# SwiGLU feed-forward on one core: interleaved tokens in the first two tiles, and the order of TensorE's waits

## The chip, the cores and the metric

The kernel runs on one core of a Trainium2 chip. The metric is the device time of one execution in microseconds (us), as a median of runs. A profile is one execution recorded by the hardware; its span goes from the first to the last instruction.

## The reference

```python
B, S, D, F = 1, 2048, 512, 1376          # x: [B, S, D], all bf16
def reference(x, w_gate, w_up, w_down):
    g = _silu(x @ w_gate)                # [S, F]
    u = x @ w_up
    return (g * u) @ w_down              # [S, D]
```

## The kernel before

The work has two halves. In the first, the hidden dimension stands on the partitions: for each chunk of 512 tokens (four chunks, `c`) and each block of 128 hidden columns (`ft`), one group of four matmuls (`dk`, the four 128-row parts of D) computes the gate, kind "G", and one the up projection, kind "U". The weights are what TensorE loads; x, transposed (`xT_sb`), streams. ScalarE applies silu to a gate group, VectorE multiplies with the up group into `hT_sb`. The 96 hidden columns left over are handled by groups of kinds "X" and "Y". In the second half, kind "O", tokens stand on the partitions: 16 tiles of 128 tokens are multiplied with w_down (matmuls on strips of 32 rows, L442, for most of it, and whole ones, L481, at the end), copied to `o_sb` by VectorE or ScalarE, and stored. There are eight `o_sb` buffers for 16 tiles.

The order on every engine is written out by hand, with semaphores. The part that matters here is the start. TensorE first runs matmuls on constants (`warm`, L354 to L356). The x of the first two tiles of 128 tokens (`NXN` = 2) is loaded plainly, rows on partitions, into `xn_sb` by `load_xn` (L113): xn0 is the first DMA on SP's queue, xn1 the second on ACT's queue, behind the first gate slab wg0. TensorE transposes these two tiles (`transposes`, L362 to L368) and VectorE and ScalarE copy the results to `xT_sb` in turn (parts 0 and 2 on VectorE, 1 and 3 on ScalarE). The x of all later tokens comes transposed by the DMA (`load_x`, L93): x0b and x0c for the rest of the first chunk, then one DMA for each further chunk.

The weights arrive in slabs of hidden blocks: block 0 (wg0, wu0), block 1 (wg1, wu1), blocks 2 and 3 (wg2, wu2), 4 to 6, and 7 to 10. The issue order on SP's queue is xn0, wu0, wg1, wu1, wg2, wu2, x0b, x0c, then the rest. TensorE takes the first eight groups (L370 to L385) in pieces as loads land: the first gate and up group on tokens 0 to 127, then on 128 to 255; then the groups at 2, 3, 4, 6, 5, 7 on tokens 0 to 255 (at 4 and 6 stand the gates of slab wg2, at 5 and 7 the ups of slab wu2); then the upper 256 tokens, which need x0b and x0c.

TensorE's waits go through `need` (L306, a load has landed) and `after` (L313, an operation of ScalarE or VectorE is done). Each weight load can carry a wait; where two stand before one weight load, the second in program order stands as an instruction of its own ahead of it.

Stores (`store_tiles`, L253) follow the order of `tiles` (L232), in which tile 0 is the fourth and tile 1 the eighth.

Of the kernel before, what the change touches and what calls it, by code (L numbers as in the profile page):

```python
# [14 lines left out]
def bass_standalone__swiglu_ffn__prompt_kernel(nc, x, w_gate, w_up, w_down, out):  # L15
    _, S, D = x.shape
    F = w_gate.shape[1]
    P = 128
# [11 lines left out]
    NXN = HT // P  # L30
    NB = 8
    NSG = 4
    NOS = 8
    SR = 32
    T01, T2, TAIL = NFF, NFF + 1, NFF + 2
    NWD = NFF + 3
    Y_ROWS = [0, 64, 0, 64]
# [4 lines left out]
    xf = x[0]  # L42
    of = out[0]
# [7 lines left out]
    with ExitStack() as es:  # L51
# [15 lines left out]
        o_sb = [sb(f"o_sb{i}", [P, D], BF16) for i in range(NOS)]  # L67
# [3 lines left out]
        xn_sb = sb("xn_sb", [P, NXN, D], BF16)  # L71
        ident = sb("ident", [P, P], BF16)

        s_I = sem("s_I")
# [6 lines left out]
        s_out = [sem(f"s_out{i}") for i in range(NOS)]  # L81
        loads = {}

        def load_sem(name):
            loads[name] = sem(f"s_{name}")
            return loads[name]
# [24 lines left out]
            load_w(eng, f"wu{a}", w_up, UPH, a * P, min(b * P, F - 32))  # L111

        def load_xn(eng, i):  # L113
            eng.dma_start(xn_sb[:, i, :], xf[i * P:(i + 1) * P, :]).then_inc(load_sem(f"xn{i}"), 16)

        def out_rows(t):
            return of[t * P:(t + 1) * P, :]

        def loads_on_scalar(act):
            load_gate(act, *slabs[0])  # L120
            load_xn(act, 1)

        def loads_on_sync(sp):
            load_xn(sp, 0)
            load_up(sp, *slabs[0])
            for a, b in slabs[1:3]:
                load_gate(sp, a, b)
                load_up(sp, a, b)
            load_x(sp, "x0b", HT, HT + P)
            load_x(sp, "x0c", HT + P, SC)  # L130
            for a, b in slabs[3:]:
                load_gate(sp, a, b)
                load_up(sp, a, b)
            load_w(sp, "wut", w_up, F - (F - 32), F - 32, F)
            for c in range(1, NSC):
                load_x(sp, f"x{c}", c * SC, (c + 1) * SC)
            sp.dma_start(
                wd_sb[:, 0:NFF, :], w_down[0:NFF * P, :].rearrange("(k p) d -> p k d", p=P)
            ).then_inc(load_sem("wd"), 16)
            load_sem("wdt")  # L140
            for y0 in (0, 64):
                sp.dma_start(wd_sb[y0:y0 + 64, T01, :], w_down[NFF * P:F - SR, :]).then_inc(loads["wdt"], 16)
            for x0 in range(0, P, SR):
                sp.dma_start(wd_sb[x0:x0 + SR, T2, :], w_down[F - SR:F, :]).then_inc(loads["wdt"], 16)
            sp.dma_start(wd_sb[0:F_LAST, TAIL, :], w_down[NFF * P:F, :]).then_inc(load_sem("wdl"), 16)
# [7 lines left out]
        def add_group(kind, **what):  # L153
            g = dict(kind=kind, at=len(groups), bank=banks[len(groups) % NB], readers=[], **what)
            groups.append(g)
            return g

        def add_op(eng, g, **what):
            n_read[eng] += 1
            op = dict(g=g, at=n_read[eng], **what)  # L160
            (act_ops if eng == "A" else dve_ops).append(op)
            g["readers"].append((eng, op["at"]))
            return op

        def tview(i, dk):
            return banks[KD * i + dk][:, 0:P // 2].bitcast(BF16)
# [26 lines left out]
        def plan_x(c):  # L193
# [4 lines left out]
            d = add_op(  # L198
                "D", g, kind="mul", out=hx_sb[X_ROWS[c]:X_ROWS[c] + SR, c, :],
                a=sgx_sb[c][96:128, :], b=g["bank"][96:128, :], after=a["at"] - 1,  # L200
# [12 lines left out]
        xt_ready = {}  # L213
        for i in range(NXN):
            for dk in range(KD):
                eng = "DA"[dk % 2]
# [16 lines left out]
        for at, t in enumerate(tiles):  # L233
            ob = at % NOS
            need = 16 * n_store[ob]
            parts = [(0, D)] if at < NST - 1 else [(0, LASTA), (LASTA, LASTB), (LASTB, D)]
            for c0, c1 in parts:
                g = add_group("O", t=t, c0=c0, c1=c1)
                eng = "A" if at % 2 == 1 and c0 == 0 else "D"
                op = add_op(  # L240
                    eng, g, kind="copy", out=o_sb[ob][:, c0:c1], src=g["bank"][:, 0:c1 - c0],
# [11 lines left out]
        def store_tiles(eng, own):  # L253
            for o, t, c0, c1, ob, copied, n in stores:
                if o == own:
                    eng.wait_ge(s_A if copied == "A" else s_D, n)
                    eng.dma_start(out_rows(t)[:, c0:c1], o_sb[ob][:, c0:c1]).then_inc(s_out[ob], 16)

        def on_sync(sp):
            loads_on_sync(sp)  # L260
            store_tiles(sp, "S")
            for i in range(NOS):
                sp.wait_ge(s_out[i], 16 * n_store[i])
# [11 lines left out]
        def on_scalar(act):  # L275
            loads_on_scalar(act)
            act.activation(adummy[:, 0:4], zero_c, ACT.Silu)  # L277
            for op in act_ops:
                act.wait_ge(*ready(op))
                if op["kind"] == "silu":  # L280
                    if op["free"]:
                        act.wait_ge(s_D, op["free"])
                    fn = ACT.Silu
                else:
                    if op["stored"][1]:
                        act.wait_ge(*op["stored"])
                    fn = ACT.Copy
                act.activation(op["out"], op["src"], fn).then_inc(s_A, 1)  # L288
            store_tiles(act, "A")
# [13 lines left out]
        def on_tensor(pe):  # L303
            landed = set()

            def need(name, count=1):  # L306
                if name not in landed:
                    pe.wait_ge(loads[name], 16 * count)
                    landed.add(name)
# [3 lines left out]
            def after(eng, n):  # L313
                if n > read[eng]:
                    pe.wait_ge(s_A if eng == "A" else s_D, n)
                    read[eng] = n
# [12 lines left out]
            def gu_needs(g, n0, n1):  # L329
                c, ft = g["c"], g["ft"]  # L330
                if c > 0:
                    need(f"x{c}")
                if c == 0 and n1 > HT:
                    need("x0b")
                if c == 0 and n1 > HT + P:
                    need("x0c")
                need(("wg" if g["kind"] == "G" else "wu") + str(slab_of[ft]))

            def gu_step(g, dk, n0, n1):
                c = g["c"]  # L340
                col = (0 if g["kind"] == "G" else UPH) + g["ft"] * P
                if c == 0:
                    for i in range(n0 // P, min(n1 // P, NXN)):
                        after(*xt_ready[i, dk])
                ins = whole(g["bank"], dk, col, c, n0, n1)
                if n1 == SC and dk == KD - 1:
                    ins.then_inc(s_P, 1)

            def gu_matmuls(g, n0, n1):
                gu_needs(g, n0, n1)  # L350
                for dk in range(KD):
                    gu_step(g, dk, n0, n1)

            def warm(n, width):  # L354
                for i in range(n):
                    pe.matmul(banks[NB - 1][:, 0:width], lhsT=ones_w, rhs=ones_m[:, 0:width], start=True, stop=True)  # L356

            warm(N_WARM, SC)
            warm(N_FILL, P)
            pe.wait_ge(s_I, 1)  # L360

            def transposes(i):  # L362
                need(f"xn{i}")
                for dk in range(KD):
                    pe.matmul(  # L365
                        tview(i, dk), lhsT=xn_sb[:, i, dk * P:(dk + 1) * P], rhs=ident[:, :],
                        start=True, stop=True, is_transpose=True,
                    ).then_inc(s_X, 1)  # L368

            first = groups[0:NB]  # L370
            transposes(0)
            warm(N_GAP, P)
            gu_matmuls(first[0], 0, P)
            transposes(1)
            gu_matmuls(first[1], 0, P)
            for dk in range(KD):
                for g in first[0:2]:
                    gu_step(g, dk, P, HT)
            for at in (2, 3, 4, 6, 5, 7):
                gu_matmuls(first[at], 0, HT)  # L380
# [6 lines left out]
            for g in groups[NB:NO]:  # L387
# [4 lines left out]
                elif kind == "X":  # L392
                    c = g["c"]
# [21 lines left out]
            def strip_of(c, k):  # L415
                spare = (P + SR - 2 * Y_ROWS[c] - X_ROWS[c]) // SR
                return (spare + k) % TPC

            def strips(q, k, fks, start, stop, turn=True):
# [7 lines left out]
                for fk in fks:  # L427
                    if fk == NFF:
                        need("wdt", 2 + TPC)
                    for c, g in zip(ORDER, quad):  # L430
                        t, c0, c1 = g["t"], g["c0"], g["c1"]
                        r0 = SR * strip_of(c, k)
                        tok = (t - c * TPC) * P
# [35 lines left out]
            for g in groups[NO + TPC * (TPC - 1):]:  # L469
                t, c0, c1 = g["t"], g["c0"], g["c1"]  # L470
# [17 lines left out]
        on_gpsimd(nc.gpsimd)  # L488
        on_scalar(nc.scalar)
        on_tensor(nc.tensor)  # L490
        on_vector(nc.vector)

# [27 lines left out]
```

## Time and profile before

| | us |
|---|---|
| median of 3 runs | 120.4 |
| the runs | 120.46, 119.94, 120.40 |
| span of the profiled execution | 118.6 |
| TensorE busy in it | 115.9 (98%) |
| VectorE busy | 38.0 (32%) |
| ScalarE busy | 35.1 (30%) |

The page gives no other time of the profiled execution than its span; the runs' times include what lies around the span, 1.8 us by the median. PE in the profile is TensorE's matmuls, PEld its weight loads, which overlap with matmuls; DVE is VectorE, ACT ScalarE, SP the queue that issues most DMAs. A "q" behind an engine's name is its sequencer, which waits and issues and is not counted as busy. The chain of waits follows the end of the span back to what released it. In the tables by stretch, the DMA share is the mean busy share of the 16 DMA engines, and values over 1 mean that packets overlap.

### The profile page before, as it was taken

How to read it: one execution, taken by the hardware profiler on the slowest of the kernel's cores; microseconds unless marked ns; L12 is line 12 of the kernel's file. 1: busy time of each engine (PE TensorE's matmuls, PEld its weight loads, DVE VectorE, ACT ScalarE, POOL GpSimd, SP SyncE). 2: the span in 40 equal slices, each digit the busy share in tenths (PEclk: the TensorE clock that was granted, in tenths of full speed). 3: DMA queues.
4: the chain of work that ended last, by engine and by line, in shares of the span. 5: the costliest groups of instructions: out<-in, count | busy, mean ns of one | idle time of the engine just before them, and what ended most of it. 6: DMA issues, size and time to landing. Idle time of an engine off the chain costs nothing.

```text
span 118.6 us, 2344 instructions
## 1 busy us (share of the span) xinstructions
PE 115.9 (98%) x1019; PEld 59.7 (50%) x1019; DVE 38.0 (32%) x60; ACT 35.1 (30%) x62; POOL 1.1 (1%) x7
## 2 busy tenths in 40 slices
PE   7999999999999999999999999999999999999993
PEld 2788444444444444444444444444444445885442
DVE  0206542444433444324444244360000044003321
ACT  3407334353244272343263432330000033003021
POOL 1000000000000000000000000010000000000000
PEclk9999999999999999999999999999999999999999
DMA  3999999991000000000000000000000017200612
GB/s 87 290 186 336 296 161 221 268 357 25 0 6 0 0 0 0 0 3 3 0 0 6 0 0 0 0 0 6 0 6 0 0 57 237 70 0 6 202 64 88
DMA packets 17642, 8.83 MB, mean 74 GB/s; under 512 B 10624, under 2 KB 17632, under 8 KB 17632
## 3 DMA queue, kind: packets, MB, share of 16 engines
q1 hardware_dynamic: 16816, 8.33, 27.3%
q10 hardware_dynamic: 816, 0.36, 1.1%
q8 instruction: 8, 0.13, 0.5%
q14 instruction: 2, 0.02, 0.0%
HBM read 4.75 MB, written 2.10 MB: 58 GB/s over the span
## 4 chain that ended last, share of the span: by engine, by line
PE 98%; DVE 0%; issue 0%
PE bank L324 62%; PE bank L442 25%; PE bank L481 7%; PE bank L356 2%; PE bank L404 2%; PE bank L365 1%; DVE o_sb L300 0%
## 5 line engine op out<-in xcount | busy, mean ns | idle before, releaser
L324 PE MATMUL bank<-xT_sb,w_sb 128*128 128x512 bf16 (+2 forms) x384 | 73.3, 352 | 0.1
L324 PEld LDWEIGHTS bank<-xT_sb,w_sb 128*128 128x128 bf16 x384 | 36.2, 98 | 36.8 <-DMA w_sb<-in_w_gate_dram 0.3
L296 DVE TENSOR_TENSOR hT_sb<-sg_sb,bank 128x512 bf16<-128x512 f32 x40 | 27.5, 688 | 40.2 <-PE bank L324 39.3
L288 ACT ACTIVATE sg_sb<-bank 128x512 f32<-128x512 f32 x40 | 23.9, 597 | 40.6 <-PE bank L324 40.5
L442 PE MATMUL bank<-wd_sb,hT_sb 32*128 32x512 bf16 x496 | 29.0, 374 | 0.0
L442 PEld LDWEIGHTS bank<-wd_sb,hT_sb 32*128 32x128 bf16 x496 | 15.2, 93 | 11.6 <-issue 0.4
L300 DVE CAST o_sb<-bank 128x512 bf16<-128x512 f32 (+1 forms) x10 | 5.7, 595 | 31.1 <-PE bank L442 25.9
L288 ACT ACTIVATE o_sb<-bank 128x512 bf16<-128x512 f32 (+1 forms) x8 | 4.3, 582 | 33.6 <-PE bank L442 27.9
L481 PE MATMUL bank<-wd_sb,hT_sb 128*128 128x512 bf16 (+2 forms) x56 | 8.1, 304 | 0.0
L481 PEld LDWEIGHTS bank<-wd_sb,hT_sb 128*128 128x128 bf16 x56 | 4.2, 98 | 4.2 <-issue 0.4
L442 PE MATMUL bank<-wd_sb,hy_sb 32*128 32x512 bf16 (+1 forms) x32 | 5.0, 371 | 0.0
L296 DVE TENSOR_TENSOR hx_sb<-sgx_sb,bank 32x512 bf16<-32x512 f32 x4 | 2.8, 692 | 3.5 <-ACT sgx_sb L288 3.5
L288 ACT ACTIVATE sgx_sb<-bank 32x512 f32<-32x512 f32 x4 | 2.4, 588 | 4.5 <-PE bank L324 4.5
L356 PE MATMUL bank<-const-bfloat16-1.0 128*128 128x512 bf16 (+1 forms) x9 | 2.8, 463 | 0.8 <-PEq L505 0.8
L442 PE MATMUL bank<-wd_sb,hx_sb 32*128 32x512 bf16 (+1 forms) x16 | 3.0, 371 | 0.0
L288 ACT ACTIVATE sgy_sb<-bank 64x512 f32<-64x512 f32 x4 | 2.4, 590 | 0.1
L356 PEld LDWEIGHTS bank<-const-bfloat16-1.0 128*128 128x128 bf16 x9 | 1.0, 128 | 2.2 <-issue 2.2
L300 DVE COPY xT_sb<-bank 128x128 bf16<-128x128 bf16 x4 | 0.8, 222 | 4.3 <-PE bank L365 4.3
L404 PE MATMUL bank<-xT_sb,w_sb 128*64 128x512 bf16 x16 | 1.9, 382 | 0.0
L442 PEld LDWEIGHTS bank<-wd_sb,hy_sb 32*128 32x128 bf16 x32 | 1.6, 93 | 0.6
L277 ACT ACT_TABLE_LOAD x1 | 1.3, 1283 | 1.9 <-issue 1.9
L404 PEld LDWEIGHTS bank<-xT_sb,w_sb 128*64 128x64 bf16 x16 | 0.8, 109 | 1.0 <-DVE hT_sb L296 0.4
(15 smaller groups left out, 6.6 us busy)
## 6 DMA issues: line engine op xcount, KB each, us to landing
out_dram<-o_sb SPq DMA_DIRECT2D x15, 128.0 KB, 1.8
wd_sb<-in_w_down_dram SPq DMA_DIRECT2D x1, 1280.0 KB, 7.3
w_sb<-in_w_gate_dram SPq DMA_DIRECT2D x1, 480.0 KB, 5.5
w_sb<-in_w_up_dram SPq DMA_DIRECT2D x1, 448.0 KB, 6.2
w_sb<-in_w_gate_dram SPq DMA_DIRECT2D x1, 384.0 KB, 4.3
w_sb<-in_w_up_dram SPq DMA_DIRECT2D x1, 384.0 KB, 4.7
w_sb<-in_w_up_dram SPq DMA_DIRECT2D x2, 128.0 KB, 3.2
w_sb<-in_w_gate_dram SPq DMA_DIRECT2D x1, 256.0 KB, 3.6
```

What stands on the lines that cost most here:

```text
L277: act.activation(adummy[:, 0:4], zero_c, ACT.Silu)
L288: act.activation(op["out"], op["src"], fn).then_inc(s_A, 1)
L296: ins = dve.tensor_tensor(op["out"], op["a"], op["b"], ALU.mult)
L300: ins = dve.tensor_copy(op["out"], op["src"])
L324: return pe.matmul(bank[:, n0:n1], lhsT=w_sb[:, dk, col:col + P], rhs=xT_sb[:, dk, c * SC + n0:c * SC + n1], start=(dk == 0), stop=(dk == ...
L356: pe.matmul(banks[NB - 1][:, 0:width], lhsT=ones_w, rhs=ones_m[:, 0:width], start=True, stop=True)
L365: pe.matmul(tview(i, dk), lhsT=xn_sb[:, i, dk * P:(dk + 1) * P], rhs=ident[:, :], start=True, stop=True, is_transpose=True,).then_inc(s_X, 1)
L404: ins = pe.matmul(g["bank"][y0:y1, :], lhsT=w_sb[:, dk, YC0:YC0 + 64], rhs=xT_sb[:, dk, c * SC:(c + 1) * SC], start=(dk == 0), stop=(dk == ...
L442: ins = pe.matmul(g["bank"][:, 0:c1 - c0], lhsT=h, rhs=wd_sb[r0:r0 + SR, w, c0:c1], start=(start and fk == fks[0]), stop=(stop and fk == f ...
L481: ins = pe.matmul(g["bank"][:, 0:c1 - c0], lhsT=h, rhs=w, start=(last and fk == 0), stop=(fk == (NFF if last else NFF - 1)), skip_group_ch ...
```

## The change

There are two edits. First, token r of each of the first two tiles no longer stands on partition r. With `SW` = 8 a row r = 8b + a stands on partition 16a + b, so that the 16 partitions from 16a on hold the rows a, a + 8, a + 16 and so on. The loads `xn0` and `xn1` read in that order, and the stores of tiles 0 and 1 write back in that order; all between treats tokens alike. Second, the order of two pairs of TensorE's waits is turned: before the first transposes, xn0's landing is now asked for ahead of the identity `s_I`; before the gate and up groups of the first chunk, the first copy of `xT_sb` is asked for ahead of the weights.

```diff
+    SW = 8
...
         def load_xn(eng, i):
-            eng.dma_start(xn_sb[:, i, :], xf[i * P:(i + 1) * P, :]).then_inc(load_sem(f"xn{i}"), 16)
-
-        def out_rows(t):
-            return of[t * P:(t + 1) * P, :]
+            rows = xf[i * P:(i + 1) * P, :].rearrange("(b a) d -> a b d", a=SW)
+            eng.dma_start(xn_sb[:, i, :], rows).then_inc(load_sem(f"xn{i}"), 16)
+
+        def out_rows(t, c0, c1):
+            rows = of[t * P:(t + 1) * P, c0:c1]
+            return rows.rearrange("(b a) d -> a b d", a=SW) if t < NXN else rows
...
-                    eng.dma_start(out_rows(t)[:, c0:c1], o_sb[ob][:, c0:c1]).then_inc(s_out[ob], 16)
+                    eng.dma_start(out_rows(t, c0, c1), o_sb[ob][:, c0:c1]).then_inc(s_out[ob], 16)
...
             def gu_matmuls(g, n0, n1):
+                if g["c"] == 0:
+                    for i in range(n0 // P, min(n1 // P, NXN)):
+                        after(*xt_ready[i, 0])
                 gu_needs(g, n0, n1)
...
             warm(N_FILL, P)
-            pe.wait_ge(s_I, 1)
...
             first = groups[0:NB]
+            need("xn0")
+            pe.wait_ge(s_I, 1)
             transposes(0)
```

## The prediction

> **What bounds the kernel now.** I read the page first, then TensorE's weight loads in order of time, then the loads' issues and landings, then the DMA's share by stretch.
>
> ```profile
> span 118.6 us, 2344 instructions
> PE 115.9 (98%) x1019; PEld 59.7 (50%) x1019; DVE 38.0 (32%) x60; ACT 35.1 (30%) x62; POOL 1.1 (1%) x7
> PE 98%; DVE 0%; issue 0%
> 6.46 71.05 PE bank L324 x360
> ```
>
> TensorE is busy for 98% of the span and carries 98% of the chain. The last row is a piece of the chain in order of time: from 6.46 us on, the gate and up matmuls run for 71 us without a wait. So a change of loads can move the end in two ways only: it changes when TensorE gets through the first 7 us, or it starves TensorE later. The sum is made against the span of 118.6 us; the median of the runs is 120.4 us, and the 1.8 us between them lie around the span, where the change puts nothing. A shift of the span is taken as the same shift of the median.
>
> The weight loads from 3.1 to 7.2 us (start, length, idle before in brackets):
>
> ```profile
> 3.24 0.35 PEld L365 LDWEIGHTS bank<-ident,xn_sb 128*128 128x128 bf16 x4 [0.16 <-issue]
> 3.91 0.36 PEld L324 LDWEIGHTS bank<-xT_sb,w_sb 128*128 128x128 bf16 x4 [0.20 <-issue]
> 4.41 0.23 PEld L365 LDWEIGHTS bank<-ident,xn_sb 128*128 128x128 bf16 x4
> 4.59 1.58 PEld L324 LDWEIGHTS bank<-xT_sb,w_sb 128*128 128x128 bf16 x20
> 6.46 0.77 PEld L324 LDWEIGHTS bank<-xT_sb,w_sb 128*128 128x128 bf16 x8 [0.28 <-DMA w_sb<-in_w_gate_dram]
> ```
>
> Who ends these waits is seen from issue and landing. Timeline of the issuing queues, then the landings (median us from issue):
>
> ```profile
> 0.81 0.40 SPq L114 DMA_DIRECT2D xn_sb<-in_x_dram  x1
> 0.81 0.47 ACTq L99 DMA_DIRECT2D w_sb<-in_w_gate_dram  x1
> 1.31 0.54 ACTq L114 DMA_DIRECT2D xn_sb<-in_x_dram  x1
> 2.83 0.51 SPq L99 DMA_DIRECT2D w_sb<-in_w_gate_dram  x1
> 3.38 0.51 SPq L99 DMA_DIRECT2D w_sb<-in_w_up_dram  x1
> ...
> xn_sb<-in_x_dram SPq DMA_DIRECT2D x1, 128.0 KB, 2.3
> xn_sb<-in_x_dram ACTq DMA_DIRECT2D x1, 128.0 KB, 3.1
> w_sb<-in_w_gate_dram ACTq DMA_DIRECT2D x1, 128.0 KB, 2.8
> w_sb<-in_w_gate_dram SPq DMA_DIRECT2D x1, 256.0 KB, 3.6
> w_sb<-in_w_up_dram SPq DMA_DIRECT2D x1, 256.0 KB, 3.8
> ```
>
> Issue plus landing: xn0 at 0.81 + 2.3 = 3.1 us (the first transposes start at 3.24), xn1 at 1.31 + 3.1 = 4.41 (the second transposes start at that moment), wg2 at 2.83 + 3.6 = 6.43 (weight loads resume at 6.46 after 0.28 us of idling), wu2 at 3.38 + 3.8 = 7.2. The eight weight loads on wg2 end at 6.46 + 0.77 = 7.23, just where wu2 lands. So wu2 is the last load that TensorE meets without slack: what comes behind it starts as much later as wu2 lands later, and starts earlier only if wu2 lands earlier.
>
> **What sets wu2's landing.** By stretches (width, PE, PEld, DVE, ACT, POOL busy, PEclk, DMA share, GB/s):
>
> ```profile
> 1.80:2.30 0.50, 0.50 (x3) 0.15 (x1) 0.00 (x0) 0.43 (x1) 0.00 (x0) 1.00 0.64 150
> 2.30:2.80 0.50, 0.50 (x2) 0.15 (x1) 0.00 (x0) 0.50 (x1) 0.00 (x0) 1.00 1.03 273
> 2.80:3.80 1.00, 1.00 (x9) 0.62 (x7) 0.23 (x2) 0.68 (x3) 0.00 (x0) 1.00 1.19 310
> 3.80:4.80 1.00, 0.94 (x13) 0.70 (x12) 0.30 (x2) 0.39 (x3) 0.00 (x0) 1.00 1.13 249
> 4.80:5.80 1.00, 1.00 (x17) 0.87 (x15) 0.24 (x2) 0.38 (x2) 0.00 (x0) 1.00 1.11 302
> 5.80:6.80 1.00, 1.00 (x10) 0.65 (x8) 0.00 (x0) 0.00 (x0) 0.00 (x0) 1.00 1.27 320
> 23.50:26.00 2.50, 2.50 (x14) 1.10 (x12) 1.38 (x2) 1.57 (x4) 0.00 (x0) 1.00 1.08 369
> ```
>
> From 2.8 us on the 16 DMA engines have more than a full share of work, until wu2 is in. Only the first microsecond has room. So wu2's landing is the sum of the DMA engines' work before it, and the most loaded engine decides.
>
> **The change, part by part.**
>
> *The two x loads.* Same 128 rows of 1 KB into the same partitions; but the source is now walked in 8 outer steps of 16 rows, where it had 128 single rows. No row of this trace has such a pattern, so it is bounded from both sides. One end: all 16 engines still share it, cost 0. Other end: the outer steps are what is shared out, then 8 engines carry both loads and 8 carry none. The price of that is read where the w_down rows, also 1 KB each, are moved: 369 GB/s at a full share (23.5 to 26.0 us). A load of 131 KB takes the 16 engines 131/369 = 0.355 us, and 8 engines 0.71 us; for two loads the eight get 2 × 0.355 = 0.71 us more work ahead of wu2, the other eight 0.71 us less. In between lies the room at the start: at the later level of about 1.15 the stretches 1.80:2.30 and 2.30:2.80 lack (1.15 - 0.64) × 0.5 + (1.15 - 1.03) × 0.5 = 0.3 us of work per engine, and the first x load, which is at the head of its queue, falls there. I take 0.71 - 0.3 = 0.4 us for wu2's landing: nearer to the eight-engine end, because the outermost count in the instruction really becomes 8 and the stretches are full from 2.8 us on.
>
> [...]
>
> A gain below nothing from the row order itself: rows that the engines read at one time lie side by side now; no row prices that, and it is kept to the rival below.
>
> The issue of a three-step pattern: the w loads, which have one step more than xn, take 0.47 to 0.51 us against 0.40 and 0.54 for xn, so within 0.1 us either way. Behind xn0 on SP's queue wait all later loads, but wg2 and wu2 are issued 3.6 and 3.8 us ahead of landing, which hides it. Behind xn1 on ACT's queue stand the table load and the first copy, which idles 0.31 us before it starts:
>
> ```profile
> 3.68 0.45 ACT L288 ACTIVATE xT_sb<-bank 128x128 bf16<-128x128 bf16 x2 [0.31 <-PE bank L365]
> L308 PEldq EVENT_SEMAPHORE  x9: 51/51/51, 3.2 to 55.4; - x9
> L315 PEldq EVENT_SEMAPHORE  x12: 51/51/51, 3.8 to 99.5; - x12
> L300 DVE COPY xT_sb<-bank 128x128 bf16<-128x128 bf16 x4 | 0.8, 222 | 4.3 <-PE bank L365 4.3
> 3.57 0.41 DVE L300 COPY xT_sb<-bank 128x128 bf16<-128x128 bf16 x2 [3.57 <-PE bank L365]
> ```
>
> *The waits.* Where two waits stand before one weight load, one becomes a wait instruction of its own (L308 in `need`, L315 in `after`, 51 ns each). Today that is the later one at two places: xn0 ahead of the first transposes (landed about 3.1, weight load at 3.24) and VectorE's first copy ahead of the first gate matmuls (copy ends 3.57 + 0.22 = 3.79, weight load at 3.91). With the order turned, the earlier one (the identity, wg0) is the separate instruction and the later one is on the weight load: between 0 and about 0.1 us less at each. I take 0.05 at the first and nothing at the second, because its second step waits for ScalarE's copy anyway (3.68 us on). Neither reaches the end: the second transposes at 4.41 wait for xn1, and behind that 0.28 us are idle before wg2. The cost of losing this cover is nil as long as wu2 decides. In the other groups of the first chunk the added `after` names operations already waited for and adds nothing. Queued behind the moved waits on TensorE is the same work as before.
>
> *The stores of tiles 0 and 1.* They are the fourth and the eighth of the first batch on SP's queue:
>
> ```profile
> 96.41 4.17 SPq L257 DMA_DIRECT2D out_dram<-o_sb  x8
> DMA to landing us min/median/max: 1.5/1.8/2.0
> 108.75 1.29 DVE L300 CAST o_sb<-bank 128x512 bf16<-128x512 f32 x2 [9.40 <-PE bank L442]
> ```
>
> All eight are issued by 96.41 + 4.17 = 100.6 us and land some 1.8 us later, 102.4. With 8 engines each takes 0.355 us more. The copies that reuse the buffers start at 108.75 us: six microseconds of cover, cost 0.
>
> *Sum.* wu2 lands 0.4 us later, at 7.6; TensorE waits there instead of meeting it; everything behind moves by 0.4 us. The loads behind wu2 have moved together with TensorE, so no new wait is expected there. 120.4 + 0.4 = 120.8 us. About 0.5% (0.6 us) is what a measurement of this kernel can tell from no change, so this forecast counts as the same.
>
> **The rivals.**
>
> *Slower, full price.* The room of the first microsecond is on the eight engines that carry no x rows. Then wu2 comes the full 0.71 us late, xn1 also, and the time is 121.1. For it: shares of 1.03 to 1.27 in all stretches from 2.3 us. Against: the first load starts alone. It decides as soon as the idle of the first stretch is not on the loaded engines.
>
> *Nothing changes.* The loads are still spread over all 16 engines: 120.4.
>
> *Faster.* A load on fewer engines is issued and started sooner, or the neighbouring rows are read faster, and wu2 too comes earlier. All that can be won is the idle time in front of TensorE: 0.16 + 0.20, then 4.41 - (3.91 + 0.36) = 0.14, then 0.28, in all 0.78 us, to 119.6. Against it: wu2 lands after a backlog that the first issue does not shorten.
>
> *Slower by the clock.* The first matmuls run at half pace:
>
> ```profile
> L356 PE MATMUL bank<-const-bfloat16-1.0 128*128 128x512 bf16 x5 | 2.3, 622 | 0.8 <-PEq L505 0.8
> L324 PE MATMUL bank<-xT_sb,w_sb 128*128 128x512 bf16 x39 | 8.6, 379 | 0.0
> ```
>
> A 128x512 matmul takes 622 ns at first and 379 ns after 10 us. If a later xn0 leaves TensorE idle so long that the full pace comes only after 7.2 us, the 1.77 us from 4.41 to 6.18 and the 0.77 us on wg2 double: 2.5 us more, less the 0.28 us idle, so 2.3 us and 122.7. Against it: the loads already leave idle time and the pace is full in good time.
>
> [...]
>
> **How the numbers follow.** Forecast (0.4 us later) 0.50; full price 0.22; no change 0.12; faster 0.10; clock 0.06. Slower by over 0.5% (past 121.0): full price 0.22, clock 0.06 and the forecast's upper tenth 0.05, together 0.33. Faster by over 0.5%: 0.10. The rest, 0.45 + 0.12 = 0.57, is the same. The range goes from the no-change case less the runs' spread below their median (119.94 to 120.4, of which I take most: 120.0) to the full price with 0.4 us for the same spread above (121.5); the clock and most of the faster case, 0.16, stay outside.
>
> **What would show it.** Right: xn1 lands after 4.4 us and wu2 near 7.6; the first weight load on wu2 has an idle time before it; the first transposes follow xn0's landing more closely than 0.1 us; no new idle time on TensorE after 9 us, and the stores of the first batch done long before 108 us. Wrong: wu2 lands at 7.2 or earlier, the span follows something other than wu2, or warm-up pace reaches past 4.6 us.

## The result and the profile after

The changed kernel takes 122.12 us (median of 4 runs, 120.85 to 122.81) against 120.43 us before (4 runs): the ratio is 1.011, with a 95% interval from 1.007 to 1.015. Four more runs later gave 122.39 us and 1.018 (1.013 to 1.023). The change makes the kernel slower by 1% to 2%, and its runs now spread over 2.4 us (120.85 to 123.20 over all eight), where those of before spread over about one. The ratios are taken over the runs within 1.5% of the fastest of their kernel, so they lie below the ratio of the medians where runs spread. The forecast was 120.8 us within 120.0 to 121.5.

The first profile of the changed kernel is of the run at 122.81 us; a second one (the last experiment) is of the run at 120.98 us. The two together split the loss. From both pages and their chains in order of time, the first profile:

```profile
span 121.5 us, 2344 instructions
1.27 4.36 DMA xn_sb<-in_x_dram
5.68 0.61 PE bank L370 x4
6.28 74.13 PE bank L327 x380
```

and the second:

```profile
span 119.7 us, 2336 instructions
1.28 4.36 DMA xn_sb<-in_x_dram
5.69 0.40 PE bank L370 x4
```

In both the second x load, 4.36 us long, stands at the start of the chain, and TensorE waits on it; before, no DMA stood in the chain. The loads are alike to 0.1 us in the two runs, and yet the spans differ by 1.8 us. So there are two losses: 119.7 - 118.6 = 1.1 us comes with the loads, and up to 1.8 us more comes with something that only some runs meet.

**The loads.** The issuing queues in the first profile, then the landings (median us from issue):

```profile
0.81 0.82 SPq L116 DMA_DIRECT2D xn_sb<-in_x_dram  x1
1.27 1.18 ACTq L116 DMA_DIRECT2D xn_sb<-in_x_dram  x1
1.69 0.43 SPq L100 DMA_DIRECT2D w_sb<-in_w_up_dram  x1
3.36 0.51 SPq L100 DMA_DIRECT2D w_sb<-in_w_gate_dram  x1
3.91 1.15 SPq L100 DMA_DIRECT2D w_sb<-in_w_up_dram  x1
w_sb<-in_w_gate_dram SPq DMA_DIRECT2D x1, 256.0 KB, 4.2
w_sb<-in_w_up_dram SPq DMA_DIRECT2D x1, 256.0 KB, 4.4
```

The two x loads hold their queues for 0.82 and 1.18 us, where they held them for 0.40 and 0.54. The weights that SP issues behind xn0 come 0.4 to 0.5 us later, and wu2 lands at 3.91 + 4.4 = 8.3 us, where it landed at 7.2. TensorE's weight loads show what became of it:

```profile
3.86 0.34 PEld L370 LDWEIGHTS bank<-ident,xn_sb 128*128 128x128 bf16 x4 [0.79 <-DMA xn_sb<-in_x_dram]
4.47 0.47 PEld L327 LDWEIGHTS bank<-xT_sb,w_sb 128*128 128x128 bf16 x4
5.67 0.34 PEld L370 LDWEIGHTS bank<-ident,xn_sb 128*128 128x128 bf16 x4 [0.73 <-DMA xn_sb<-in_x_dram]
5.97 3.03 PEld L327 LDWEIGHTS bank<-xT_sb,w_sb 128*128 128x128 bf16 x21
```

xn0 is met 0.62 us later than before (3.86 against 3.24), xn1 1.26 us later (5.67 against 4.41), each after some three quarters of a microsecond of idling. Behind xn1 it waits for no load for more than 0.1 us, in either profile; in the second, wg2 and wu2 have just landed when it comes to them.

**The pace.** The last of these rows, cut at 9 us, holds 21 weight loads in 3.03 us; in the second profile 35 of them stand in 3.21 us:

```profile
5.87 3.21 PEld L327 LDWEIGHTS bank<-xT_sb,w_sb 128*128 128x128 bf16 x35
```

By stretches of 1 us (columns as in the prediction), the first profile

```profile
2.80:3.80 1.00, 0.55 (x3) 0.15 (x1) 0.00 (x0) 0.99 (x2) 0.00 (x0) 1.00 0.66 197
8.60:9.60 1.00, 1.00 (x7) 0.71 (x5) 0.00 (x0) 0.00 (x0) 0.00 (x0) 1.00 0.50 56
9.70:10.70 1.00, 1.00 (x11) 0.90 (x10) 0.00 (x0) 0.00 (x0) 0.00 (x0) 1.00 0.97 293
```

and the second:

```profile
8.60:9.60 1.00, 1.00 (x15) 0.92 (x13) 0.00 (x0) 0.00 (x0) 0.00 (x0) 1.00 0.60 53
```

Between 8.6 and 9.6 us 5 weight loads fall in the first profile and 13 in the second; TensorE counts as fully busy in both, and only the counts give it away. After 9.7 us the first is up to 10. It had worked at half pace until then; in the second, and in the kernel before, half pace ended before 5 us. What half pace is, the start and a later piece of the chain show. The weight loads of the wide matmuls on constants begin 0.42 to 0.43 us apart (1.22, 1.65, 2.08, 2.50 and 2.93 us in the first profile) and take 147 ns each; later they take 98 ns, and 49 wide matmuls take 10.74 us, 0.22 us each (second profile):

```profile
23.83 10.74 PE bank L327 x49
```

The PEclk column says 1.00 throughout: it does not show this state. The first row of the first profile, from 2.8 to 3.8 us, shows a DMA share of 0.66, where it was 1.19: the 16 engines run short of work just when the queues are held by the issue.

**How many engines.** The packets of the page, changed kernel:

```profile
DMA packets 17610, 8.83 MB, mean 73 GB/s; under 512 B 10592, under 2 KB 17600, under 8 KB 17600
q1 hardware_dynamic: 16792, 8.33, 27.8%
q10 hardware_dynamic: 808, 0.36, 1.1%
```

and before:

```profile
DMA packets 17642, 8.83 MB, mean 74 GB/s; under 512 B 10624, under 2 KB 17632, under 8 KB 17632
q1 hardware_dynamic: 16816, 8.33, 27.3%
q10 hardware_dynamic: 816, 0.36, 1.1%
```

The same megabytes take 32 packets fewer, 24 on SP's queue (three of the copies) and 8 on ACT's (one). That is 8 fewer for each of the four interleaved copies, as if 8 engines in place of 16 reported its end. No view shows the engines of one copy: where engines of a copy are counted below, that is the author's inference from the packets. The runs that follow fit it: 17626 packets where two copies are interleaved (experiments five and eight), 17642 with 16 outer steps in place of 8 (three), and 17594, 12 fewer for each copy, with 4 (thirteen).

### The profile page after: what moved, and what is told of

The parts are those of the page before. It is cut to its first block, busy times and chain, and to the rows that moved or that the text cites. A ratio compares the mean times of both kernels' runs of the same rounds, so it can differ in the third digit from the quotient of the medians.

```text
span 121.5 us, 2344 instructions
## 1 busy us (share of the span) xinstructions
PE 117.8 (97%) x1019; PEld 61.3 (50%) x1019; DVE 38.1 (31%) x60; ACT 35.2 (29%) x62; POOL 1.1 (1%) x7
## 4 chain that ended last, share of the span: by engine, by line
PE 94%; DMA 4%; ACTq 0%; DVE 0%; issue 0%
PE bank L327 61%; PE bank L449 24%; PE bank L488 7%; DMA xn_sb<-in_x_dram 4%; PE bank L411 2%; PE bank L370 0%; ACTq L100 0%; DVE o_sb L303 0%
## 5 line engine op out<-in xcount | busy, mean ns | idle before, releaser
L327 PE MATMUL bank<-xT_sb,w_sb 128*128 128x512 bf16 (+2 forms) x384 | 75.0, 360 | 0.0
L327 PEld LDWEIGHTS bank<-xT_sb,w_sb 128*128 128x128 bf16 x384 | 37.6, 101 | 36.9
L370 PE MATMUL bank<-ident,xn_sb 128*128 128x128 bf16 x8 | 1.2, 306 | 1.1 <-DMA xn_sb<-in_x_dram 1.1
```

The source lines that it names most:

```text
L327: return pe.matmul(bank[:, n0:n1], lhsT=w_sb[:, dk, col:col + P], rhs=xT_sb[:, dk, c * SC + n0:c * SC + n1], start=(dk == 0), stop=(dk == ...
L370: pe.matmul(tview(i, dk), lhsT=xn_sb[:, i, dk * P:(dk + 1) * P], rhs=ident[:, :], start=True, stop=True, is_transpose=True,).then_inc(s_X, 1)
```

## The experiments

Three theories were to be told apart. Load theory: the interleaved loads land late, because eight engines carry them (engine theory) or because they hold the queues longer (issue theory). Clock theory: TensorE, idling for them, stays at half pace longer. Wait theory: the turned waits cost.

**One: the waits alone.** Before with the edits in `gu_matmuls` and ahead of `transposes(0)`, the loads and stores plain.

> Before, with TensorE's two pairs of waits turned and nothing else. Load theory (two loads on eight engines land late) and clock theory (TensorE idles for them and stays at half pace longer) both put all of the loss on the loads: 120.4 us, ratio 0.997 to 1.003, with the first transposes about 0.05 us closer to xn0's landing. Wait theory (the turned waits cost): the loss of 1.3 to 1.7 us shows here, 121.7 or more.

Measured: 120.11 us (12 runs) against 120.40; ratio 0.9998 (0.9977 to 1.0019). The waits cost nothing and bring nothing that can be told.

**Two: the interleaving alone.** The changed kernel with the old order of waits.

> Before, with the interleaved loads and stores and the old order of waits. Load and clock theories: as slow as the full change, 121.7 to 122.2 us, with the same spread of over 1 us between runs. Wait theory: 120.4 us.

Measured: 122.28 us (6 runs, 121.67 to 122.84), ratio 1.016 (1.012 to 1.020). The whole loss is in the interleaving. The profile, of a run at 122.68 us, has the late pace too, 22 weight loads up to 9 us where the second profile of the full change has 35, with wu2 at 3.94 + 4.3 = 8.2 us as there:

```profile
5.83 3.25 PEld L327 LDWEIGHTS bank<-xT_sb,w_sb 128*128 128x128 bf16 x22
```

**Three: sixteen outer steps.**

```diff
-    SW = 8
+    SW = 16
```

> The full change with SW = 16 in place of 8: the tokens are interleaved as well, but the outermost count is 16, which 16 DMA engines can share. If the eight engines are the cause: xn0 and xn1 are issued in 0.4 to 0.55 us again, land at 3.1 and 4.4 us, and the time is 120.4 us (ratio 0.997 to 1.003). If interleaved rows are slow by themselves (their order, or the pattern's third step): issue stays near 0.8 and 1.2 us and the time near 122 us.

Measured: 120.88 us (12 runs), ratio 1.0044 (1.0021 to 1.0066). Neither expectation holds. The packets are 17642 again, so by the same count 16 engines report; but the loads still hold their queues longer than plain ones, and wu2 lands at 3.87 + 4.4 = 8.3 us, as late as in the full change:

```profile
0.81 0.68 SPq L116 DMA_DIRECT2D xn_sb<-in_x_dram  x1
1.26 0.65 ACTq L116 DMA_DIRECT2D xn_sb<-in_x_dram  x1
3.87 0.60 SPq L100 DMA_DIRECT2D w_sb<-in_w_up_dram  x1
w_sb<-in_w_up_dram SPq DMA_DIRECT2D x1, 256.0 KB, 4.4
7.52 1.53 PEld L327 LDWEIGHTS bank<-xT_sb,w_sb 128*128 128x128 bf16 x15 [0.50 <-DMA w_sb<-in_w_gate_dram]
```

So a late wu2 does not need eight engines. What SW = 16 is spared is the long wait for xn1, which lands at 1.26 + 3.3 = 4.6 us in place of 5.6. Here TensorE waits for wg2 (last row) and not for xn1, and the span of 119.7 us is that of the full change's second profile.

**Four: the idle time filled.** The changed kernel with matmuls on constants where TensorE idles.

```diff
-N_FILL = 2
+N_FILL = 9
+N_MID = 7
...
+            warm(N_MID, P)
             transposes(1)
```

> The full change, with more matmuls on constants where TensorE idles for the two loads: 7 more before the first transposes and 7 before the second (128 columns each, 107 ns at half pace). They leave the landings alone. Clock theory: the full pace comes near 3.5 us in most runs, wu2 at 8.3 us is what remains, and the time falls to 121.0 to 121.5 us with a spread below 0.7 us. Load theory alone (the landings explain all, the clock is a by-product): no change against the full change, 121.7 to 122.2 us.

Measured: 121.14 us (11 runs, 120.80 to 121.52), ratio 1.0057 (1.0035 to 1.0080). Useless work in the gaps wins back about 1 us and takes the spread from 2 us to 0.7. That is the clock theory's outcome; load theory alone expected no change. The profile, of a run at 121.41 us, is at full pace from 4.6 us on, and wu2 lands at 3.92 + 4.8 = 8.7 us.

**Five: tile 1 alone interleaved.**

```diff
-            rows = xf[i * P:(i + 1) * P, :].rearrange("(b a) d -> a b d", a=SW)
+            rows = xf[i * P:(i + 1) * P, :]
+            if i == 1:
+                rows = rows.rearrange("(b a) d -> a b d", a=SW)
...
-            return rows.rearrange("(b a) d -> a b d", a=SW) if t < NXN else rows
+            return rows.rearrange("(b a) d -> a b d", a=SW) if t == 1 else rows
```

> The full change with the second tile alone interleaved (its load on ACT's queue and its store), the first tile plain. Issue theory (an interleaved load holds its queue 0.4 to 0.6 us longer, and what is issued behind it comes later): SP's queue is undisturbed, xn0 lands at 3.1 us, wu2 at 7.2 to 7.4, xn1 near 5.2; 120.4 to 120.9 us. Engine theory (eight engines carry too much): half of the extra work, wu2 at 7.5 to 7.7, 120.7 to 121.0 us. If the clock is lost by the idling before xn1 alone, 121.3 us or more.

Measured: the 11 runs fall in two groups with nothing between, five at 120.52 to 120.97 us and six at 122.17 to 122.94; median 122.17, ratio 1.0065 (1.0022 to 1.0107), which stands for neither group. SP's queue is undisturbed, and yet wu2 lands at 3.42 + 4.2 = 7.6, 0.4 us later than before: the landing that engine theory named, where issue theory had 7.2 to 7.4. In the profile of nine it lands at 7.6 again; plain loads issued in time landed at 7.2 three times (before, one, eight) and 7.4 once (six). The DMA share falls to 0.78 between 3.8 and 4.8 us (1.13 before), with all weights up to wu2 issued by 3.93. The profile is of a run at 122.22 us; TensorE waits 0.97 us for xn1 and is at half pace until 8.6:

```profile
1.31 1.19 ACTq L118 DMA_DIRECT2D xn_sb<-in_x_dram  x1
5.49 0.35 PEld L372 LDWEIGHTS bank<-ident,xn_sb 128*128 128x128 bf16 x4 [0.97 <-DMA xn_sb<-in_x_dram]
3.80:4.80 1.00, 0.81 (x6) 0.32 (x4) 0.15 (x1) 0.56 (x4) 0.00 (x0) 1.00 0.78 195
7.60:8.60 1.00, 1.00 (x6) 0.75 (x5) 0.00 (x0) 0.00 (x0) 0.00 (x0) 1.00 0.73 133
8.80:9.80 1.00, 1.00 (x12) 0.89 (x10) 0.00 (x0) 0.00 (x0) 0.00 (x0) 1.00 0.79 233
```

**Six: idling with the loads untouched.** The kernel of experiment one with fewer warm-up matmuls.

```diff
-N_WARM = 5
+N_WARM = 3
```

> Before with the turned waits, and three wide matmuls on constants at the start where it had five: TensorE idles some 0.85 us before xn0 (as the full change makes it do), all loads as before. Clock theory: the full pace comes later in part of the runs, median 120.8 to 122.5 us with a wide spread. If idling there does nothing to the pace: 120.1 to 120.5 us.

Measured: 121.20 us (11 runs, 119.91 to 121.86), ratio 1.0043 (1.0009 to 1.0077). The loads land about as before (wu2 at 3.37 + 4.0 = 7.4), and still the spread is 2 us. The profiled run, at 121.30 us, is at half pace until 8.0:

```profile
3.22 0.34 PEld L367 LDWEIGHTS bank<-ident,xn_sb 128*128 128x128 bf16 x4 [1.00 <-DMA xn_sb<-in_x_dram]
7.00:8.00 1.00, 1.00 (x7) 0.69 (x6) 0.00 (x0) 0.00 (x0) 0.00 (x0) 1.00 1.19 160
8.10:9.10 1.00, 1.00 (x12) 0.89 (x10) 0.00 (x0) 0.00 (x0) 0.00 (x0) 1.00 0.55 117
```

In this run one microsecond of idling at the start costs 1.4 us of span (120.0 against 118.6), with wu2 0.2 us late; the median moves by 0.9 us, and some runs lose nothing.

**Seven: plain rows, issued later.** The kernel of experiment one with a load of 2 KB, used by nobody, ahead of each x load.

```diff
...
+        def load_tiny(eng, j):
+            eng.dma_start(tiny[0:16, j, :], xf[j * 16:(j + 1) * 16, 0:64]).then_inc(load_sem(f"tiny{j}"), 16)
...
+            load_tiny(act, 1)
             load_xn(act, 1)
...
+            load_tiny(sp, 0)
             load_xn(sp, 0)
...
```

> Before with the turned waits, and one added load of 2 KB that nobody uses at the head of SP's queue and one ahead of xn1 on ACT's. xn0 and all behind it is issued some 0.45 us later on each queue, with plain rows on 16 engines and next to no work more. Issue theory: wu2 lands 0.3 to 0.6 us later, at 7.5 to 7.8, and the time is 120.7 to 121.6 us (more where the clock is hit too). Engine theory: the backlog hides the issue, wu2 lands at 7.2 to 7.35 and the time is 120.1 to 120.6 us.

Measured: 121.29 us (11 runs, 120.67 to 122.53), ratio 1.0071 (1.0042 to 1.0100). In the profile (the run at 120.67 us) the DMA share from 2.8 to 3.8 us falls to 0.66, just as in the full change, and wu2 lands at 3.85 + 4.2 = 8.05 us:

```profile
1.27 0.41 SPq L115 DMA_DIRECT2D xn_sb<-in_x_dram  x1
1.85 0.44 ACTq L115 DMA_DIRECT2D xn_sb<-in_x_dram  x1
3.85 0.60 SPq L100 DMA_DIRECT2D w_sb<-in_w_up_dram  x1
w_sb<-in_w_up_dram SPq DMA_DIRECT2D x1, 256.0 KB, 4.2
2.80:3.80 1.00, 0.66 (x5) 0.26 (x4) 0.00 (x0) 0.99 (x2) 0.00 (x0) 1.00 0.66 136
```

Half a microsecond of issue (wu2 at 3.85 in place of 3.38 us), with plain rows, delays its landing by 0.85 us, more than the 0.3 to 0.6 us that issue theory gave it; the backlog hides nothing.

**Eight: the stores alone.** The changed kernel with plain loads; the output's rows of tiles 0 and 1 come out permuted.

```diff
-            rows = xf[i * P:(i + 1) * P, :].rearrange("(b a) d -> a b d", a=SW)
+            rows = xf[i * P:(i + 1) * P, :]
```

> The turned waits and the interleaved stores of tiles 0 and 1; the loads are plain, so that in these two tiles the output's rows come out permuted. All theories: the stores are hidden, 120.1 to 120.5 us (ratio 0.997 to 1.003). If the stores hold SP's queue long enough to meet the buffers' reuse, 120.8 us or more.

Measured: 120.16 us (10 runs), ratio 0.9987 (0.9963 to 1.0010). The stores cost nothing. The profiled run, the slowest at 120.76 us, has plain loads with wu2 at 7.2 us, and still a late pace: after 0.34 us of idling for xn1 it gets through 37 weight loads from 4.88 to 9.08 us, where the profile of experiment one has 51 from 4.58 to 9.06.

**Nine to eleven: the idle time filled in five, seven and three.** Nine adds `warm(12, P)` ahead of `transposes(1)` to experiment five; ten has `N_FILL = 6` and `warm(5, P)` in experiment seven; eleven has `N_FILL = 6` in experiment three.

> The kernel with tile 1 alone interleaved, with 12 narrow matmuls on constants before the second transposes, where TensorE idled about 1.3 us. Its runs without them fell in two groups, five at 120.5 to 121.0 and six at 122.2 to 122.9 us. [...] If the two groups come from the loads (their landings differ from run to run): both groups stay.

> Plain rows with the added small loads ahead of xn0 and xn1, and the idle time filled with narrow matmuls (4 more before the first transposes, 5 before the second). Issue theory with the clock taken out: about 0.45 us of issue moves wu2 by 0.4 to 0.9 us, 120.7 to 121.2 us, spread below 0.7 us. If the earlier 121.3 us was the clock alone: 120.1 to 120.4 us.

> The full change with SW = 16 and 4 more narrow matmuls before the first transposes. Issue theory: the three-step pattern still holds the queues 0.68 and 0.65 us, wu2 near 8.0, 120.6 to 121.0 us as without the fill (120.9), without the one slow run at 122. If the 0.5 us of SW = 16 was the clock: 120.1 to 120.4 us.

Measured: nine 120.81 us (11 runs, 120.47 to 121.55, ratio 1.0052, 1.0033 to 1.0071); ten 121.06 us (5 runs, 121.01 to 121.41, ratio 1.0073, 1.0048 to 1.0099); eleven 120.69 us (11 runs, 120.50 to 121.34, ratio 1.0042, 1.0025 to 1.0059). In nine the upper group is gone, though wu2 lands at 7.6 as in five; but four of the runs lie above 121.0 us (121.15 to 121.55), and the profiled one, the slowest at 121.55 us, still has a late pace: its weight loads take 147 ns until 6.9 us, with gaps of no more than 0.27 us since 3.1. In ten and eleven the tail of times above 121.5 us is gone, and what stays, 0.4% to 0.7%, goes with the later landing of wu2: at 3.84 + 4.7 = 8.5 us in the profile of ten and 3.87 + 3.9 = 7.8 in that of eleven. The same loads landed at 8.05 in seven and 8.3 in three, so a landing read from one profile is good to about half a microsecond.

**Twelve: an earlier issue.** The kernel of experiment one with wg1 on ACT's queue, so that wu1, wg2 and wu2 are issued 0.55 us earlier: an attempt to get below both kernels.

```diff
             load_xn(act, 1)
+            load_gate(act, *slabs[1])
...
-                load_gate(sp, a, b)
+                if a > 1:
+                    load_gate(sp, a, b)
```

> Before with the turned waits, and wg1 issued on ACT's queue behind xn1 instead of on SP's, so that wu1, wg2 and wu2 are issued some 0.55 us earlier. Issue theory in the other direction: wu2 lands 0.1 to 0.4 us earlier and the time falls to 119.8 to 120.1 us, below before's 120.4. If the engines' backlog alone sets wu2: wu2 stays at 7.2 and the time is 120.2 to 120.5 us. If ScalarE's later first copy counts: 120.5 us or more.

Measured: 120.76 us (11 runs), ratio 1.0035 (1.0012 to 1.0057): slower, and no better version. wu2 is issued at 2.81 and lands 4.8 us later, at 7.6. Issue theory does not hold in this direction. The chain and the weight loads show where the time goes: wg1, on ACT's queue, takes 4.29 us to land, and TensorE waits 0.49 us for it, where before it was in time.

```profile
1.85 4.29 DMA w_sb<-in_w_gate_dram
6.18 7.76 PEld L326 LDWEIGHTS bank<-xT_sb,w_sb 128*128 128x128 bf16 x73 [0.49 <-DMA w_sb<-in_w_gate_dram]
```

That the loads, issued earlier, hold each other up is a guess that no run tests.

**Thirteen: four outer steps, filled.** The edit is shown against experiment four.

```diff
-N_FILL = 9
-N_MID = 7
+N_FILL = 14
+N_MID = 10
...
-    SW = 8
+    SW = 4
```

> The full change with SW = 4: the outermost count is 4, so 4 engines carry the two x loads, 32 rows of 1 KB each, and idle time is filled with 12 narrow matmuls more before the first transposes and 10 before the second. Engine theory: at 0.355 us for a load on 16 engines, four engines get 2 x 3 x 0.355 = 2.1 us more work ahead of wu2, which lands at 9 us or later; 122 us or more. Issue theory (the count of engines matters only through the time on the queue): the issue takes 0.8 to 1.3 us, wu2 lands at 8.2 to 8.7 us; 121.0 to 121.6 us. In the packets' count each of the four copies shows 12 completions fewer than before: 17642 - 48 = 17594.

Measured: 122.58 us (4 runs), ratio 1.0169 (1.0138 to 1.0201). Packets 17594, as expected. The x loads hold the queues no longer than with SW = 8, but wu2 lands at 3.84 + 5.2 = 9.0 us:

```profile
0.81 0.77 SPq L117 DMA_DIRECT2D xn_sb<-in_x_dram  x1
1.27 1.11 ACTq L117 DMA_DIRECT2D xn_sb<-in_x_dram  x1
3.84 2.27 SPq L101 DMA_DIRECT2D w_sb<-in_w_up_dram  x1
w_sb<-in_w_up_dram SPq DMA_DIRECT2D x1, 256.0 KB, 5.2
1.27 5.42 DMA xn_sb<-in_x_dram
```

So the number of outer steps has a price beside the issue time, which engine theory names and puts on the engines. With the issue time unchanged, xn1 takes 5.42 us with SW = 4 (last row, from the chain) where it takes 4.36 with SW = 8, and wu2 lands 0.3 to 0.7 us behind two landings with SW = 8, 8.7 in experiment four and 8.3 in the full change.

**Fourteen: the full change once more.**

> The full change again, unaltered, for more runs of it. [...]

Measured: 120.98, 122.02, 122.75 and 123.20 us, ratio 1.018 (1.013 to 1.023). The profile is of the run at 120.98 us, shown above: full pace before 5.9 us, wu2 at 3.92 + 4.3 = 8.2 us. The runs spread as widely as in the first set, but eight runs from 120.85 to 123.20 do not show two clean groups, as they did for tile 1 alone.

## Why the prediction was wrong

*What bounds the kernel: right in the sum, not in the wait.* The span less wu2's landing is 111.3 to 111.6 us in nine of the ten profiles in which the last weight load of 147 ns ends before 6.2 us: 7.2 us with a span of 118.6 before, 8.05 with 119.4 in experiment seven, 8.3 with 119.7 in three, 8.2 with 119.7 in the full change's second profile, and likewise in one, four, ten, eleven and twelve; the tenth, thirteen, has 112.1. In the other six half pace lasts past 6.5 us, and it is 112.3 to 113.4.

But the wait is not where the prediction put it. It expected idle time before the first weight load on wu2; the full change has it before xn1. xn1 had 0.28 us of slack (the idle time before wg2) and came 1.26 us later, and outside the rival of full price the prediction gave it no cost. With the prediction's 1.77 and 0.77 us of weight loads behind xn1, TensorE reaches wu2 at 5.68 + 2.54 = 8.2 us, just as wu2 lands, so the profile can't tell which of the two sets the end. Later weights alone are enough (experiment three). For a late xn1 alone there is an estimate: in experiment five 5.49 + 2.54 + 111.4 gives a span of 119.4 and a time near 120.7 us, where its five faster runs lie (120.52 to 120.97); wu2 at 7.6 would give 120.3.

*The x loads: the right direction, mis-sized.* wu2 was put 0.4 us later and came 1.1 us later. Two terms of that step failed. The first is the issue, "within 0.1 us either way" and hidden by the 3.6 and 3.8 us between issue and landing: it grew by 0.42 and 0.64 us, and experiment seven shows that such a delay alone, with next to no work added, costs 0.85 us of landing (1.3 in the profile of ten). The time from issue to landing was read as slack; in experiment seven, with 4.2 us of it, it hid none of the delay. The second is the room of 0.3 us at the start: the share of 0.66 between 2.8 and 3.8 us, where it was 1.19, shows some 0.5 us less work done by each engine at the start, not more. That eight outer steps put a load on eight engines was the author's estimate; the runs show its packets, 8 fewer for each copy, and its time. A price beside the issue is there too: four steps cost more than eight at the same issue time (thirteen, wu2 at 9.0 us against 8.7 and 8.3), and in experiment five one load in eight steps goes with a wu2 0.4 us later, near the prediction's 0.355 us, though wu2 is issued within 0.04 us of before; only xn1's own longer issue is left there as another cause. How the 1.1 us of the full change divides into issue and engines is not told: filled, SW = 16 and SW = 8 stand at 1.0042 (1.0025 to 1.0059) and 1.0057 (1.0035 to 1.0080), with overlapping intervals.

*The clock: the rival with 0.06 was the larger half.* Its mechanism came as described, half pace past 7.2 us after idling for the x loads, and its price of 2.3 us was near the measured 1.8 between two runs with the same landings. The step that failed is the argument against it, that "the loads already leave idle time and the pace is full in good time". Idle times of 0.16 and 0.20 us had been survived; 0.79 and 0.73 were not, in most runs. Experiments four, six and nine show it from both sides: filling the gaps removes most of the loss (121.14 us in four; 120.81 in nine, 122.17 unfilled), making a gap without touching the loads brings 0.9 us of median (121.20 in six). How much idle time is too much is not shown: the profiled runs of eight and nine are late with gaps of 0.34 us and less, and that of seven is in time with gaps of 0.60 and 0.41. Nor is it shown what delays the pace in one run and not in another of the same kernel: the two profiles of the full change idle alike, 0.79 and 0.73 us in the one, 0.81 and 0.74 in the other, and half pace lasts past 8.6 us in the first and ends before 5.9 in the second.

*The waits, the stores, later loads: right.* Ratios of 0.9998 and 0.9987, and no wait on a load in the chain after xn1, in either profile of the full change.

*The sum.* The prediction took the 1.8 us between the span of 118.6 and the median of 120.4 to lie around the span. In every run whose span is on record time and span differ by 1.2 to 1.3 us; so by that difference the profiled execution before belongs to a run near 119.9 us, at the fast end of that kernel, and 118.6 is fairly set against the fast end after. For the second profile 118.6 + 1.1 = 119.7 us of span, 120.98 us of time; for the first, with its late pace, 119.7 + 1.8 = 121.5 and 122.81. The median lies between them; that most of the eight runs lost part of the pace is inferred from their times, since only the two were profiled. The range left the clock outside as 6 chances in 100.

*Still open.* Why 0.46 us of issue becomes 0.85 us or more of landing; how much of wu2's 1.1 us is issue and how much engines; how much of the 0.8 and 1.2 us of issue is the third step of the pattern and how much the number of outer steps (16 steps: 0.68 and 0.65); and how much idle time, at which place, delays the full pace in a given run.

## What to carry to other kernels

In this kernel the issue time of the first DMAs was on the path although wu2 lands some 4 us after its issue: in experiment seven 0.46 us more of it moved the landing by 0.85 us. Where a kernel starts with its loads in a queue, look at the DMA share of the first stretches (0.66 in place of 1.19 here), and price every change of a pattern's steps by its hold on the queue (0.82 and 1.18 us in place of 0.40 and 0.54). Idle time of TensorE in the first microseconds was not worth its own length here: in experiment six 1.00 us of it went with half pace until 8.0 us and 1.4 us more span in one run, while the runs of that kernel spread from 119.91 to 121.86 us. So look at the spread of the runs and at the count of weight loads per microsecond (5 against 13 from 8.6 to 9.6 us), not at busy shares (1.00 in both). Matmuls on constants that bridge a known wait were a cheap test of this, and most of a remedy: 121.14 us in experiment four, where the two sets of the full change had 122.12 and 122.39.

## What was not expected of the hardware

A load of 128 rows of 1 KB holds its queue for 0.40 and 0.54 us (SP, ACT) as plain rows, 0.68 and 0.65 us as 16 interleaved steps, 0.82 and 1.18 us as 8, and 0.77 and 1.11 us as 4. The second x load takes 3.0 to 3.3 us from issue to landing as plain rows, 3.3 to 3.7 as 16 steps, 4.4 as 8 and 5.4 as 4. A later, ordinary load can be held too: wu2's issue took 0.51 us before, 1.03 to 1.22 us in three profiles with eight steps and 2.27 us with four; but 0.58 in experiment four, also with eight, and 0.83 in eleven with sixteen, so it does not hang on the number of steps alone.
